# Operands of a routing search moved from SBUF to PSUM or to a per-partition scalar, in a kernel of attention and two mixtures of experts

## The chip, the cores and the metric

One core of a Trainium2 chip runs the whole program. The metric is device time in microseconds for one execution, from the inputs in HBM to the outputs in HBM. The core's engines are TensorE (PE in the rows), VectorE (DVE), ScalarE (ACT), GpSimd (POOL) and SyncE (SP), each with a queue of its own that it works off in order.

## The reference

Three layers run one after the other; what matters here is the third and how it assigns tokens.

```python
def _attn_ref(q, k, v, alpha):           # 4 x 8 heads, 768 tokens, 48 wide
    for t in range(S):
        state = alpha[:, :, t, :, None] * state + einsum('bhd,bhe->bhde', k[:, :, t], v[:, :, t])
        y[:, :, t] = einsum('bhd,bhde->bhe', q[:, :, t], state)

def _moe_ref(x, w_in, w_out):            # 3072 tokens, 384 -> 2048 -> 384
    h = np.maximum(x @ w_in, 0.0)
    return h * h @ w_out

def _moe2_ref(x, w_gate, w1, w2):        # 8 experts, 384 -> 1024 -> 384
    cap = N // E                         # 384 tokens for each expert
    logits = x @ w_gate
    for idx in np.argsort(-logits.flatten()):
        tok, e = idx // E, idx % E
        if assigned[tok] >= 0 or counts[e] >= cap: continue
        assigned[tok] = e; counts[e] += 1
    for e in range(E):
        h = np.maximum(x[assigned == e] @ w1[e], 0.0)
        out[assigned == e] = h @ w2[e]
```

The greedy loop goes through all pairs of token and expert from the greatest logit down; an expert with 384 tokens is closed.

## The kernel before

The first 597 us or so are attention and the first mixture, which the change does not touch. Then comes the routing, and with it, interleaved, the eight routed experts.

**The routing** works in phases, one for each expert that fills up (`search`, line 801). The logits `L` lie in SBUF as 128 partitions x 24 chunks x 8 experts. A phase looks for the greatest threshold at which some open expert would have 384 tokens whose best open logit is at or above it. It does so in 5 rounds (`ITERS`), each with 32 thresholds (`T`) in a finer grid:

- `thr` (line 827): the 32 thresholds, the round's grid `iot` plus the per-partition numbers `n` and `at`; in the first round they are the grid itself;
- `cm` (line 829): which of a partition's 24 tokens are at or above each threshold, 768 comparisons a partition of `m2` with `thr`, both spread by steps of zero;
- `pc` (838, TensorE): six products of `cm` with `oh`, each token's best expert, that count the tokens; `rc` (841) takes the counts to SBUF;
- `pb` (851): TensorE adds the blocks up; `full` (854) compares with what the experts still take; `pb` (856) counts how many thresholds are full, and `steps` (865) makes the next `n` of it;
- `at` (861): in the third and fourth round, one element a partition, the thresholds' offset so far plus `n`;
- in the second round `ee` (844) multiplies `oh` with the experts' numbers, both in SBUF, and in the third `ei` (847) adds that up.

Behind the fifth round, `hi` (869) is the threshold found, `a` (873) marks the tokens above it, and `aid` (874, a copy under the mask `a`) gives them their expert's number. TensorE's `pz`, then `cl`, `cz`, `ez` and `ek` (879 to 884) name the expert that closed; `mk`, `mi` and `wi` (885, 886, 705) list its tokens and where its weights lie, from which its weights (`w1s`, `w2s`) and, after `slots`, its tokens (`xg`) are fetched by indirect DMA from GpSimd's queue. `na` (896) takes the assigned tokens out of the next phase.

**The experts.** Each has 8 steps; a step is `layer1` (`ph`, line 957, nine products) and `layer2` of two steps before (`py`, line 975, three times three products). Weights and tokens are split into a high and a low part for float32 accuracy: ScalarE makes the high parts of the weights (line 920), GpSimd (or VectorE, where the plan says d) subtracts them from the whole to get the low ones (`wbuf`, line 922), with both inputs in SBUF; these come in short bursts. `xt` (931, 932) does the same for the tokens, on ScalarE and VectorE, out of PSUM.

**What sets the order.** From line 631 on, TensorE, VectorE, ScalarE and GpSimd work in the order of the program text. Tables written out by hand (`START`, `FIRST`, `STEADY`, `EXTRA` and their like, lines 51 to 82) say behind which product of an expert's step a piece of the search (`s`), of the slots (`t`), of the weights' split (`h` on ScalarE, `p` on GpSimd, `d` on VectorE) or of the tokens (`x`) is issued. So while expert e runs, phase e + 2 is searched, and a product for `pc` stands in TensorE's queue between those of the expert: what makes `cm` late makes the expert late.

**PSUM** has eight banks: three with the tag a (`bank("a", ...)`, line 96), taken in turn by the routing's tiles and the tokens' transposes, two for `ph`, three for `py`. Before the change `thr`, `at` and `a` lie in SBUF; a round's bank for `pc` is taken just before its products.

Of the kernel before, what the change touches and what calls it, by code (L numbers as in the profile page):

```python
# [7 lines left out]
F32 = mybir.dt.float32  # L8
# [5 lines left out]
OP = mybir.AluOpType  # L14
# [6 lines left out]
E, F2 = 8, 1024  # L21
CAP = N // E
C = 128
NCH = N // C
# [24 lines left out]
# what each step of an expert does beside its products: s the search of a phase after the next, t the slots  # L49
# of the next, h, p, d weights' parts, x tokens, e, w the former expert's results  # L50
# [37 lines left out]
def moe_kernel(ctx: ExitStack, tc: tile.TileContext, akq, v, w_in, w_out, w_gate, w1, w2, out,  # L88
# [14 lines left out]
    # the last chunk's rows come after one of zeros  # L103
# [14 lines left out]
    # attention inputs of one chunk of 128 tokens: decays, keys and queries with a pair of heads' columns in the  # L118
    # partitions, a column of zeros after each pair's tokens, and values with the tokens in the partitions
# [3 lines left out]
    def load(ch, parts=((0, 3),), eng=sp):  # L123
        """the rows between a pair's heads take the second's first, for whatever is finite will do"""
        for lo, hi in parts:
            for p0, n, r0 in ((0, 64, 0), (64, 48, 48)):
                eng.dma_start(nat[ch % 2][p0:p0 + n, lo:hi, :, :C], akq[ch, r0:r0 + n, lo:hi])
# [4 lines left out]
    # constants that the first chunk needs  # L132
# [30 lines left out]
    # constants that depend on shapes alone  # L163
# [45 lines left out]
    XF, XT = {}, {}  # L209

    def back(x):
        """a row's elements, the last one first"""
        n = x.shape[-1]
        return bass.AP(tensor=x.tensor, offset=x.offset + n - 1, ap=[list(a) for a in x.ap[:-1]] + [[-1, n]])

    def attn(ch, tags="aaaaa"):
        """yields after each of its parts: a decays, q queries and keys, s scores, n keys back, o results"""
# [7 lines left out]
        # products of the decays from each token on, and up to each token over the whole chunk's; what each pair's  # L225
        # start from comes in where the zeros are
# [41 lines left out]
        def result(lo, hi):  # L268
            """what some pairs of heads give, in one bank"""
            py = bank(next(tag), "py")  # L270
            o = py.rearrange("p (a t) -> p a t", a=NP)
            for p in range(lo, hi if c else lo):
                pe.matmul(o[:, p], sa[:, p], qt[:, p], start=p == lo, stop=False)
            for p in range(lo, hi):
                for j in range(2):
                    pe.matmul(o[64 * j:64 * j + D, p], vn[:, 2 * p + j], Pt[:, j, p, :],
                              start=not c and p == lo, stop=p == hi - 1)
            for h in ((slice(0, 128),) if c and hi == NP else (slice(0, D), slice(64, 64 + D))):
                act.activation(x[h, lo:hi, cu * C:(cu + 1) * C], v4(py)[h, lo:hi], AF.Copy)
            if cu == CPU - 1 and hi == NP:  # L280
                # the last pair of heads fills the rows that the other pairs leave
                for o in (0, 64):
                    sp.dma_start(x[o + 48:o + 64, :KT, :], x[o:o + 48, KT, :])
# [63 lines left out]
    def narrow(dst, src):  # L347
        """float64 words (low, high) to float32, of which dst takes the bits"""
# [82 lines left out]
    def gate(dst, x):  # L431
        """x's rows times the gate's weights"""
# [5 lines left out]
    def gate_w():  # L438
        """w_out's rows times the gate's weights"""
# [9 lines left out]
    def share(n):  # L449
        """n steps of what the vector engine does for the gate"""  # L450
        while n and tasks:
            if next(tasks[-1], "end") == "end":
                tasks.pop()
            else:
                n -= 1

# [14 lines left out]
    def start_conv(n=1):  # L471
        """the next conversions, in turns so that none waits for itself"""
# [44 lines left out]
    def logit_range():  # L517
        """the lowest of the logits, but for the last unit's, and what scales them from there to 0..T"""
# [25 lines left out]
    def attend(g):  # L544
        """attention's parts that go with step g"""
# [11 lines left out]
    def first_step(g):  # L557
        """a step of the first unit, whose weights come along"""
# [71 lines left out]
    # the rest, in the order of this text  # L630
# [3 lines left out]
    def last_unit():  # L634
        """the last unit's second layer, three products at a time"""
# [50 lines left out]
    # logits of the last unit  # L686
# [33 lines left out]
    def load_half(h):  # L720
        """half of the second layer's weights, for the first expert"""
# [10 lines left out]
    def slots(k, mk, mi, part=False):  # L732
        """token of each of the 384 slots of the expert whose tokens mk marks; mi counts them in a partition;
        in part: the last chunk's are not gathered but marked"""
# [57 lines left out]
    def prep(k):  # L792
        """what a phase's search starts from"""
# [7 lines left out]
    def search(k):  # L801
        """one phase: the greatest threshold with which an expert is full, that expert and its tokens"""
# [20 lines left out]
        for it in range(ITERS):  # L823
            thr = iot[:, 0]
            if it:
                thr = sm.tile([128, T], F32, name="thr", bufs=2)
# [8 lines left out]
            # G chunks at a time, of which the blocks on the diagonal count  # L835
            pc = bank("a", "pc")
# [22 lines left out]
            elif 1 < it < ITERS - 1:  # L859
                at2 = sm.tile([128, 1], F32, name="at", bufs=2)  # L860
                dve.tensor_tensor(at2, at, n, op=OP.add)  # L861
# [5 lines left out]
        # the threshold as the last comparison had it  # L867
# [4 lines left out]
        a = sm.tile([128, NCH], F32, name="a", bufs=2)  # L872
# [37 lines left out]
    def split_w(k, i, e="hp"):  # L910
        """a part of an expert's weights: three of the first layer's, four of the second's"""
# [22 lines left out]
    def first_x():  # L934
        """the first expert's tokens: those of the last chunk from where they are, and the others as they come"""
# [114 lines left out]
    # whether each phase closed one expert and each expert has its 384 tokens  # L1050
# [29 lines left out]
    def across(x, row, negate=False):  # L1080
        """the greatest of a column's values, in every partition"""
# [7 lines left out]
    def total(x, n):  # L1089
        """the sums of n columns over the partitions, in every partition"""  # L1090
# [6 lines left out]
    def general_phase(L2, gum, gaid, gcap, tok, idr):  # L1097
# [19 lines left out]
        # tokens with the same first choice that come before each token  # L1117
# [16 lines left out]
        # the last token of each expert that fills up, and the first of these tokens  # L1134
# [22 lines left out]
        # the tokens up to that one get their first choice  # L1157
# [59 lines left out]
def arrays(inputs):  # L1217
    """the inputs as the chip reads them"""
    import numpy as _np

    # a chunk's tokens last, a pair's heads before the pairs
# [3 lines left out]
    # rows in the order in which the attention's results come  # L1225
# [30 lines left out]
```

## Time and profile before

| | us |
|---|---|
| median of 3 runs | 973.15 |
| lowest and highest run | 966.78 and 974.82 |
| span of the profiled execution, for which no other time is given | 973.9 |
| busy in it: TensorE | 833.9 |
| busy in it: VectorE | 714.5 |
| busy in it: GpSimd | 443.2 |
| busy in it: ScalarE | 327.7 |

The span runs from the first to the last instruction of one execution. Busy times say how much of it an engine was at work, not who was waited for. An instruction that is held while it runs, by another engine's use of a port for instance, counts as busy: in the rows a long duration of a small instruction is such a hold. A timeline row gives the start, the duration, the engine, the line, the operation, its output and inputs, and in brackets the idle time before it and what ended that. Neighbouring instructions of one kind are merged into one row, with their number.

### The profile page before, as it was taken

What the parts mean: (1) busy time and instruction counts of PE and PEld (TensorE: products, weight loads), DVE (VectorE), ACT (ScalarE), POOL (GpSimd) and SP (SyncE); (2) the same over time, 40 slices, a digit from 0 to 9 for tenths busy, and PEclk for the clock granted to TensorE, in tenths of its full rate; (3) what the DMA queues carried; (4) which work ended last, traced back from release to release, by engine and by line L of the source; (5) the groups of instructions that cost most, each with busy time, mean ns of one, the idle gap of its engine ahead of it and who ended that gap; (6) DMA issues with size and microseconds to landing.
All of it is one profiled execution on the core that took longest, in us unless ns stands there. A gap on an engine that the chain in (4) does not pass through costs nothing.

```text
span 973.9 us, 14629 instructions
## 1 busy us (share of the span) xinstructions
PE 833.9 (86%) x5583; PEld 759.1 (78%) x5583; DVE 714.5 (73%) x1594; ACT 327.7 (34%) x581; POOL 443.2 (46%) x389
## 2 busy tenths in 40 slices
PE   6868779888979889899999999748788797988974
PEld 6658678877878779899999998647677685777974
DVE  6878998999998999958542134777687787875540
ACT  1344533223123223233343352224242442425521
POOL 2386763353454444433342442343464556644431
PEclk7888989999999999999999999958798898988988
DMA  9763543112122122232300000314042240422400
GB/s 208 156 190 107 164 110 70 37 28 61 38 43 62 37 43 61 37 72 56 58 25 1 7 25 13 134 37 155 1 178 102 77 171 9 178 84 96 179 25 27
DMA packets 51484, 76.98 MB, mean 79 GB/s; under 512 B 3409, under 2 KB 42706, under 8 KB 49362
## 3 DMA queue, kind: packets, MB, share of 16 engines
q1 hardware_dynamic: 21570, 27.24, 10.3%
q0 software_dynamic: 5520, 34.61, 9.6%
q10 hardware_dynamic: 24320, 14.16, 7.7%
q8 instruction: 45, 0.74, 0.3%
q14 instruction: 29, 0.24, 0.1%
HBM read 65.27 MB, written 9.54 MB: 77 GB/s over the span
## 4 chain that ended last, share of the span: by engine, by line
PE 40%; DVE 36%; issue 4%; ACT 4%; DMA 1%; POOL 1%; POOLq 0%; DVEq 0%; ACTq 0%
DVE gj L435 15%; PE ph L390 9%; PE p L414 7%; PE ph L957 7%; PE py L975 7%; DVE at L861 3%; PE p L641 3%; DVE s L400 3%; DVE wbuf L922 2%; ACT wbuf L920 2%; DVE A L232 1%; DVE thr L827 1%; DVE cm L829 1%; DVE suf L229 1%; DVE Pt L261 1%
## 5 line engine op out<-in xcount | busy, mean ns | idle before, releaser
L390 PE MATMUL ph<-xT,wbuf 128*128 128x384 f32 x1152 | 234.6, 348 | 29.5 <-DVE s L400 12.0
L390 PEld LDWEIGHTS ph<-xT,wbuf 128*128 128x128 f32 x1152 | 207.5, 192 | 40.4 <-DVE s L400 17.4
L402 POOL TENSOR_TENSOR hl<-s,hl 128x384 fp32r<-128x384 f32 x112 | 141.8, 1266 | 184.9 <-ACT hl L401 171.2
L414 PE MATMUL p<-wbuf,hl 128*128 128x384 f32 (+1 forms) x1008 | 205.4, 348 | 4.9 <-POOL hl L402 2.7
L414 PEld LDWEIGHTS p<-wbuf,hl 128*128 128x128 f32 x1008 | 180.0, 193 | 12.2 <-issue 4.2
L975 PE MATMUL py<-wbuf,hl 128*128 128x384 f32 x576 | 133.6, 364 | 0.0
L957 PE MATMUL ph<-xt,wbuf 128*128 128x384 f32 x576 | 122.5, 358 | 10.3 <-DVE xt L932 5.9
L400 DVE SCALAR_TENSOR_TENSOR s<-ph,s 128x384 f32<-128x384 f32 x112 | 62.0, 553 | 89.2 <-ACT s L395 88.8
L401 ACT ACTIVATE hl<-s 128x384 fp32r<-128x384 f32 x112 | 58.8, 525 | 195.7 <-DVE s L400 193.8
L957 PEld LDWEIGHTS ph<-xt,wbuf 128*128 128x128 f32 x576 | 103.7, 198 | 14.1 <-DVE xt L932 6.7
L975 PEld LDWEIGHTS py<-wbuf,hl 128*128 128x128 f32 x576 | 105.6, 201 | 0.7
L435 DVE SCALAR_TENSOR_TENSOR gj<-gx,wg 128x384 f32<-128x384 f32 x128 | 96.1, 751 | 3.1
L395 ACT ACTIVATE s<-ph 128x384 f32<-128x384 f32 x128 | 62.1, 486 | 100.2 <-PE ph L390 70.5
L435 DVE SCALAR_TENSOR_TENSOR gj<-xo,wg 128x384 f32<-128x384 f32 x120 | 78.3, 652 | 12.9 <-ACT xo L422 10.5
L965 ACT ACTIVATE hl<-ph 128x384 fp32r<-128x384 f32 x64 | 31.7, 496 | 135.6 <-PE ph L957 118.6
L922 POOL TENSOR_TENSOR wbuf<-w2s,wbuf 128x768 fp32r<-128x768 f32 x28 | 53.3, 1925 | 44.1 <-ACT wbuf L920 44.1
L966 DVE SCALAR_TENSOR_TENSOR hl<-ph,hl 128x384 fp32r<-128x384 f32 x64 | 35.4, 553 | 38.3 <-ACT hl L965 37.4
L920 ACT ACTIVATE wbuf<-w1s 128x1024 fp32r<-128x1024 f32 x24 | 52.2, 2227 | 2.3 <-DMA w1s<-in_moe_w_dram,wi 2.3
L983 POOL DMA_INDIRECT out_dram<-o,idx x24 | 29.8, 1243 | 50.9 <-ACT o L980 19.0
L838 PEld LDWEIGHTS <-cm 128*128 128x128 bf16 x210 | 8.1, 100 | 49.9 <-DVE cm L829 46.3
L838 PE MATMUL pc<-oh,cm 128*128 128x32 bf16 x210 | 11.3, 182 | 40.1 <-DVE cm L829 40.1
L729 POOL DMA_INDIRECT xg<-x2d,row x24 | 25.1, 1046 | 38.7 <-DVE idx L785 18.2
(204 smaller groups left out, 1229.8 us busy)
## 6 DMA issues: line engine op xcount, KB each, us to landing
rawi<-in_moe_w_in_dram SPq DMA_DIRECT2D x16, 384.0 KB, 3.5
rawo<-in_moe_w_out_dram SPq DMA_DIRECT2D x16, 384.0 KB, 3.7
akq<-in_akq_dram ACTq DMA_DIRECT2D x16, 384.0 KB, 4.5
akq<-in_akq_dram ACTq DMA_DIRECT2D x16, 288.0 KB, 5.8
x2d<-xo SPq DMA_DIRECT2D x24, 192.0 KB, 2.0
v<-in_v_dram ACTq DMA_DIRECT2D x16, 192.0 KB, 2.5
akq<-in_akq_dram SPq DMA_DIRECT2D x7, 384.0 KB, 5.8
akq<-in_akq_dram SPq DMA_DIRECT2D x7, 288.0 KB, 7.3
```

Of the source, the lines that this page charges most:

```text
L390: pe.matmul(ph[:, :UT], win[:, wi, kt, fs], XT[u][:, xi, kt, :], start=n == 0, stop=n == 3 * KT - 1)
L395: act.activation(s, ph[:, :UT], AF.Relu)
L400: dve.scalar_tensor_tensor(s, ph[:, :UT], 0.0, s, op0=OP.max, op1=OP.mult)
L401: act.activation(hl[:, 0], s, AF.Copy)
L402: (dve if (u, f) == (NU - 1, FT - 1) else pool).tensor_tensor(hl[:, 1], s, hl[:, 0].bitcast(F32), op=OP.subtract)
L414: pe.matmul(PY[u][t][:, :w], hl[:, si, t * C:(t + 1) * C], wout[:, wi, f, :w], start=f == 0 and n == 0, stop=f == FT - 1 and n == 2)
L435: dve.scalar_tensor_tensor(junk, x, 1.0, wg[:, e], op0=OP.mult, op1=OP.mult, accum_out=dst[:, e:e + 1])
L920: act.activation(dst[:, 0], src, AF.Copy)
L922: (dve if "d" in e else pool).tensor_tensor(dst[:, 1], src, dst[:, 0].bitcast(F32), op=OP.subtract)
L957: pe.matmul(ph[:, :CAP], wa[:, wi, kt, j, :], xt[:, xi, kt, :], start=n == 0, stop=n == 3 * KT - 1)
L966: dve.scalar_tensor_tensor(hl[:, 1], ph[:, :CAP], 0.0, hl[:, 0].bitcast(F32), op0=OP.max, op1=OP.subtract)
L975: pe.matmul(PX[k, i][:, :DM], hl[:, hi_, i * 128:(i + 1) * 128], wb[:, wi, j, :], start=j == 0 and n == 0, stop=j == FT2 - 1 and n == 2)
```

## The change

Four operands of the search move; everything is computed as before.

- `thr` lies in the round's PSUM bank `pc`, in the 32 columns behind those of the counts, and the bank is taken at the start of the round.
- `cm` thereby compares `m2` in SBUF with `thr` in PSUM.
- `at` is made by a `tensor_scalar`, with `n` as a per-partition scalar, in place of a `tensor_tensor` with two tensor inputs.
- `a` lies in the last round's bank `pb`, behind the columns of the counts; `aid` and `na` read it there.

```diff
         for it in range(ITERS):
+
+            pc = bank("a", "pc")
             thr = iot[:, 0]
             if it:
-                thr = sm.tile([128, T], F32, name="thr", bufs=2)
+                thr = pc[:, G * E:G * E + T]
                 dve.tensor_scalar(thr, iot[:, it], n, at, op0=OP.add, op1=OP.add)
             cm = sm.tile([128, NCH, T], BF, name="cm", bufs=2)
             dve.tensor_tensor(cm, m2[:, :, None].to_broadcast([128, NCH, T]),
...
             yield
-            pc = bank("a", "pc")
             for c in range(0, NCH, G):
...
                 at2 = sm.tile([128, 1], F32, name="at", bufs=2)
-                dve.tensor_tensor(at2, at, n, op=OP.add)
+                dve.tensor_scalar(at2, at, n, None, op0=OP.add)
                 at = at2
...
-        a = sm.tile([128, NCH], F32, name="a", bufs=2)
+        a = pb[:, 2 * E:2 * E + NCH]
         dve.tensor_scalar(a, m2, hi, None, op0=OP.is_ge)
         dve.copy_predicated(aid, a.bitcast(mybir.dt.uint32), ei)
```

The rest of the diff takes comments out. No instruction moves: every engine has as many as before, in the same order, and only the operands of those above differ. Behind the changed lines the numbers go up by one (`cm` is line 831, `at` 862, `a` 874 and `aid` 875 of the kernel after).

## Rows read from the trace of the kernel before

**Rows 1.** Page, part 4: share of the chain that ended last, by engine.

```profile
PE 40%; DVE 36%; issue 4%; ACT 4%; DMA 1%; POOL 1%; POOLq 0%; DVEq 0%; ACTq 0%
```

**Rows 2.** Waits from 628 us on: us in total, times, longest us.

```profile
PE pc L838 <- DVE cm L829: 40.1, 11, 9.7
...
PE pp L736 <- DVE wi L705: 3.2, 6, 1.0
```

**Rows 3.** Instructions of three tiles: ns min/median/max, first and last start us, forms.

```profile
L861 DVE TENSOR_TENSOR at<-n x7: 138/6627/6705, 608.7 to 847.7; 128x1 f32<-128x1 f32 x7
...
L827 DVE TENSOR_SCALAR thr<-iot,n,zero x7: 300/302/8439, 601.9 to 839.1; 128x32 f32<-128x32 f32 x7
...
L829 DVE TENSOR_TENSOR cm<-m,thr x28: 957/958/3540, 602.3 to 860.6; 128x768 bf16<-128x768 f32 x28
```

**Rows 4.** Timeline of the first of four like stalls: start us, us, what.

```profile
723.69 5.82 POOL L922 TENSOR_TENSOR wbuf<-w1s,wbuf 128x1024 fp32r<-128x1024 f32 x2
724.11 0.56 DVE L932 TENSOR_TENSOR xt<-px,xt 128x384 fp32r<-128x384 f32 x1 [0.45 <-ACT xt L931]
...
724.66 6.63 DVE L861 TENSOR_TENSOR at<-n 128x1 f32<-128x1 f32 x1
...
729.46 1.80 POOL L922 TENSOR_TENSOR wbuf<-w2s,wbuf 128x768 fp32r<-128x768 f32 x1
...
732.76 0.34 PE L838 MATMUL pc<-oh,cm 128*128 128x32 bf16 x6 [5.38 <-DVE cm L829]
...
736.82 2.10 PE L957 MATMUL ph<-xt,wbuf 128*128 128x384 f32 x9
```

**Rows 5.** A subtraction of 384 columns with both inputs in SBUF, GpSimd idle.

```profile
L402 DVE TENSOR_TENSOR deferred<-s,deferred x1: 559/559/559, 593.5 to 593.5; 128x384 fp32r<-128x384 f32 x1
```

**Rows 6.** Timeline of the next burst on GpSimd, and of VectorE beside it.

```profile
737.89 5.83 POOL L922 TENSOR_TENSOR wbuf<-w2s,wbuf 128x768 fp32r<-128x768 f32 x3 [6.62 <-ACT wbuf L920]
...
739.96 0.18 DVE L841 CAST rc<-pc 128x32 f16<-128x32 f32 x1
...
741.52 0.27 DVE L869 TENSOR_SCALAR hi<-n,at 128x1 f32<-128x1 f32 x1
...
741.84 1.92 DVE L873 TENSOR_SCALAR a<-m,hi 128x24 f32<-128x24 f32 x1
...
744.75 0.17 DVE L883 SCALAR_TENSOR_TENSOR ez<-cz,ioe 128x8 f32<-128x8 f32 x1
```

**Rows 7.** Window behind the stall: busy us by engine, PEclk, DMA share, GB/s.

```profile
734.00:736.80 2.80, 2.80 (x14) 1.91 (x12) 1.13 (x3) 1.30 (x3) 0.00 (x0) 0.50 0.00 0
```

**Rows 8.** Timeline of the same products at the full clock, one expert earlier.

```profile
693.14 0.32 PE L838 MATMUL pc<-oh,cm 128*128 128x32 bf16 x6
...
695.59 1.83 PE L957 MATMUL ph<-xt,wbuf 128*128 128x384 f32 x9
```

**Rows 9.** Timeline of the stall in the expert before that.

```profile
678.69 6.08 POOL L922 TENSOR_TENSOR wbuf<-w1s,wbuf 128x1024 fp32r<-128x1024 f32 x2 [1.65 <-ACT wbuf L920]
...
679.34 2.68 DVE L827 TENSOR_SCALAR thr<-iot,n 128x32 f32<-128x32 f32 x1
...
682.05 3.54 DVE L829 TENSOR_TENSOR cm<-m,thr 128x768 bf16<-128x768 f32 x1
684.70 2.57 POOL L922 TENSOR_TENSOR wbuf<-w2s,wbuf 128x768 fp32r<-128x768 f32 x1
...
685.65 0.34 PE L838 MATMUL pc<-oh,cm 128*128 128x32 bf16 x6 [5.81 <-DVE cm L829]
...
689.18 3.25 PE L957 MATMUL ph<-xt,wbuf 128*128 128x384 f32 x9
```

**Rows 10.** Timeline of the first stall, before the first expert's products.

```profile
633.80 8.44 DVE L827 TENSOR_SCALAR thr<-iot,n,zero 128x32 f32<-128x32 f32 x1
...
636.87 5.31 POOL L922 TENSOR_TENSOR wbuf<-w2s,wbuf 128x768 fp32r<-128x768 f32 x3
...
643.77 0.35 DVE L844 TENSOR_TENSOR ee<-oh,ioe 128x192 f32<-128x192 bf16 x1
```

## The prediction

> **What bounds the kernel now.** I read the chain of waits first. TensorE has 40% of it and VectorE 36% [rows 1]: for long stretches the end is set by VectorE. The change touches the routing alone, which begins some 375 us before the end, so the waits of that stretch came next. There TensorE waits 40.1 us in 11 pieces for `cm`, the comparison with which each round of the search begins, the longest 9.7 us; and 3.2 us in 6 pieces for `wi`, which stands behind the end of a search [rows 2].
>
> Why is `cm` late? The list of durations answers it [rows 3]. The sum `at` is one element a partition; its shortest run took 138 ns, and its median is 6,627 ns. `thr` goes from 300 to 8,439 ns, `cm` from 957 to 3,540 ns. Nothing in their sizes differs; something holds them. The timeline of one expert shows what [rows 4]: GpSimd begins three subtractions of weight parts (`wbuf`) at 723.69 and ends the last at 729.46 + 1.80 = 731.26; `at`, begun at 724.66, ends at 731.29. In that burst `xt`, with one input in PSUM and one in SBUF, took 0.56 us, what the same size takes with both inputs in SBUF and nobody beside it (559 ns, [rows 5]). In the next burst, from 737.89 to 743.72, `rc` (from PSUM to SBUF) took 0.18 us and `hi` 0.27 us, while `a`, with 24 elements, was held for 1.92 us, to the end of that burst [rows 6]. So what is held has two tensor inputs in SBUF (`at`, `cm`), or is a `tensor_scalar` from SBUF to SBUF with more than one element (`thr`, `a`). What passes has an input in PSUM (`xt`, `rc`), or is a one-element `tensor_scalar` with per-partition scalars (`hi`).
>
> The Trainium skill (SBUF — State Buffer, Who interferes with whom) says this as a rule: VectorE and GpSimd share a pair of ports, taken for a whole instruction by a VectorE instruction with two SBUF inputs or one in a two-port mode. The trace agrees, with 6.63 us for one element.
>
> **The change part by part.** The order of the instructions is the same on every engine; only where operands lie changes. `at` becomes the kind of instruction that `hi` is. `thr` writes PSUM, which no row shows for an SBUF input; its bounds are 0.30 us, the free run, and a hold as today. I take the free run: its mirror image `rc`, with only the other side in PSUM, is the nearest row and passes. `cm` takes one input from PSUM and becomes the kind that `xt` is: free, at 0.96 us. `a` and `aid` likewise. What remains as it was is `ee`, two SBUF inputs, once a search.
>
> *The four steady stalls.* `at` is held in four experts (at 724.66, 765.8, 806.7 and 847.7 us), and each time TensorE waits some 5.38 us for `cm` [rows 4]. TensorE is done with its products at 732.76 − 5.38 = 727.38. Without the hold `at` ends at 724.9, `steps` and `thr` take half a microsecond and `cm` ends by 726.8: before TensorE asks. The wait goes whole. Its cost goes on behind it, because TensorE comes out of it at a granted clock of 0.50, the 1.2 GHz level [rows 7]. From the products for `pc` to the next expert's first `ph` it then takes 736.82 − 732.76 = 4.06 us; the same products at the full clock, an expert earlier, took 695.59 − 693.14 = 2.45 [rows 8]. That is 1.61 us, and 2.10 − 1.83 = 0.27 on `ph` itself. Per expert 5.38 + 1.61 + 0.27 = 7.26; four times, 29.0.
>
> What is late next? That `ph` needs the parts GpSimd is still making. Its first two subtractions end at 723.69 + 5.82 = 729.51; TensorE will be there at 727.38 + 2.45 = 729.83. So the wait stays away by 0.3 us, and GpSimd is the next bound. The second burst waits for ScalarE, which follows TensorE, and moves along.
>
> *The stall at 679.* `thr` waits for GpSimd's first subtraction, `cm` for its second, and `cm` ends at 685.59; TensorE has waited 5.81 us, since 679.84 [rows 9]. Free, `thr` and `cm` take 679.34 + 0.30 + 0.03 + 0.96 = 680.6, and 0.95 us of waiting is left with the semaphores: 4.86 saved. The clock: 689.18 − 685.65 = 3.53 against 2.45, and `ph` 3.25 against 1.83, together 2.50. But GpSimd's two subtractions end at about 678.69 + 5.8 = 684.5, and `ph` would be due at 680.8 + 2.45 = 683.25; some of its products can go ahead, so 0.9 us is given back. 4.86 + 2.50 − 0.9 = 6.5.
>
> *The stall at 633.8.* Here `thr` is held 8.44 us, through GpSimd's burst up to 636.87 + 5.31 = 642.18 [rows 10]. Free, `cm` would end near 635.1 and TensorE's products and `rc` near 635.6. Then comes `ee`, which still has two SBUF inputs, in the middle of the same burst. `full` and all further products of TensorE stand behind it. If it is held to the end of the burst it ends at 642.53; before it ended at 643.77 + 0.35 = 644.12: a gain of 1.6 us. If it gets in at the first change of instruction (636.87), the gain is 644.12 − 636.87 − 0.3, less a little, or 7.0 us. I take 1.6: `thr` missed three such changes in this very burst (before each of the last three subtractions), and `at` missed two in each of its four.
>
> *The end of a search.* `a` and `aid` no longer hold `wi`. TensorE's 3.2 us there [rows 2] don't go whole, since `pz` and `hl` stand in between: half, 1.5.
>
> *Costs.* `cm`'s 768 columns against the 384 of [rows 5] give (957 − 559) / 384 = 1.04 ns a column; were `thr` to pay that in full for its 32 columns on top of what it costs today, it would be 33 ns a round, under 1 us in all, and mostly hidden beside TensorE's products. A page speaks against the change here: the Trainium skill (VectorE: DVE Perf Modes, The TRN2 errata) gives VectorE a fixed 120 cycles from PSUM against 58 from SBUF. By that, an estimate, some 65 ns on each `thr` and `cm` of some 24 rounds among the experts is 3 us, and the sum would end near 938. The rows differ: 0.56 us with PSUM [rows 4] against 0.559 without [rows 5]. I take nothing, neither a loss nor a gain.
>
> Sum: 29.0 + 6.5 + 1.6 + 1.5 = 38.6. From the span of the profiled execution, 973.9 us, that leaves 935.3. The median of the three runs is 973.15, 0.1% below the span, so no correction: 935 us.
>
> **Rivals.**
>
> *The hold lasts one GpSimd instruction only.* Then `ee` passes at 636.87, the first stall gives 7.0 in place of 1.6, and the time is 930. For it: at 679 `thr` and then `cm` got in between two of GpSimd's instructions, and GpSimd's third took 2.57 us there [rows 9] against 1.80 [rows 4]. Against: the eight changes that `at` missed. The Trainium skill (SBUF — State Buffer, Who interferes with whom) has the loser blocked until the first finishes; [rows 4] show it blocked past two finishes.
>
> *GpSimd, or a slow clock, keeps half of it.* The margin before `ph` is 0.3 us. If the subtractions lengthen, if `ez` (two SBUF inputs), which began 744.75 − 743.72 = 1.03 us behind the second burst's end [rows 6] and comes closer as `a` gets shorter, runs into that burst at one subtraction, 1.8 us, a time, or the clock stays low so that the 10 us counted for it don't come, it costs 4 × 1.8 = 7 and up to 10 us: 942 to 952, 947 in the middle. For it: how thin the margins are.
>
> *`thr` is held even with its output in PSUM.* Then `at` passes but `thr` ends where `at` did, at 731.3 + 0.3, and `cm` at 732.6, where it ended at 732.7. The steady stalls stay. What is left is `cm` at 682.05, 3.54 − 0.96 = 2.6, and part of 1.5: 970, no change that can be told. Against it: `rc`.
>
> *Slower: `cm` reads PSUM slowly.* Its second input repeats 32 PSUM columns 24 times, which no row shows. The gain is used up from 38.6 / 24 = 1.6 us more on each of the 24 `cm` among the experts, so from 2.6 us each. At four times the present 0.96 it would be 24 × 2.88 = 69 us, and the time 973.9 − 38.6 + 69 = 1004. Against it: `xt` reads 384 PSUM columns at the usual pace.
>
> **How the numbers follow.** My forecast has 0.55, the shorter hold 0.20, half kept 0.15, `thr` still held 0.06, the slow read 0.04. The first three are faster by over 1% (below 963.4, about what a measurement of this kernel can tell from no change): 0.90. The fourth is the same, 0.06, the last slower, 0.04. The range goes down to 926, which is 930 with the 3 us of TensorE's shorter waits for `cm` (40.1 − 9.7 − 5.8 − 4 × 5.4) and the 0.9 given to GpSimd, and up to 952, the third case's upper end.
>
> **What would show it.** In the list of durations `at`, `thr`, `cm`, `a` and `aid` should have maxima near their medians. TensorE's wait for `cm` should fall from 40.1 to under 12 us, and the four pieces of 5.4 should be gone, with the granted clock at 1.00 behind them. `ee` (0.35 us where nothing holds it, [rows 10]) should have one run of over 6 us near 636, which is new; if it is about 1.3 us, the first rival is right. I am wrong if `thr` shows runs of several microseconds again, if `cm` is over 1.1 us, or if the waits for `cm` go and the time stays above 955.

## The result, and the profile after

The kernel after takes 926.84 us (median of 4 runs, 924.29 to 930.47), the kernel before 973.99 us beside it (4 runs, 966.78 to 977.53): a ratio of 0.9546, with a 95% interval of 0.9493 to 0.9598. A ratio, here and below, is to runs of the kernel before that were taken beside it, from undisturbed runs alone, so it is not the quotient of the two medians. The forecast was 935 us, 926 to 952. The profiled execution's span fell from 973.9 to 924.4 us.

I read the same views as before. First the chain by engine, from the page of the kernel after, part 4; against [rows 1] VectorE's share falls from 36% to 31%:

```profile
PE 41%; DVE 31%; ACT 6%; issue 3%; DMA 2%; POOL 1%; POOLq 0%; ACTq 0%; DVEq 0%
```

The waits from 628 us on (total, times, longest), against [rows 2]:

```profile
PE pc L839 <- DVE cm L831: 5.3, 6, 1.6
...
PE pp L736 <- DVE wi L705: 1.6, 6, 0.3
```

TensorE's wait for `cm` went from 40.1 to 5.3 us, and no piece of 5.4 us is left. The durations (ns, min/median/max), against [rows 3]:

```profile
L829 DVE TENSOR_SCALAR pc<-iot,n,zero x7: 314/314/315, 600.9 to 799.5; 128x32 f32<-128x32 f32 x7
...
L831 DVE TENSOR_TENSOR cm<-m,pc x28: 953/954/955, 601.2 to 814.3; 128x768 bf16<-128x768 f32 x28
...
L845 DVE TENSOR_TENSOR ee<-oh,ioe x7: 348/348/608, 603.7 to 801.3; 128x192 f32<-128x192 bf16 x7
...
L862 DVE TENSOR_SCALAR at<-n x7: 192/192/193, 607.7 to 808.1; 128x1 f32<-128x1 f32 x7
...
L875 DVE COPY_PREDICATED aid<-pb,ei x7: 186/188/190, 616.0 to 818.2; 128x24 f32<-128x24 uint32 x7
```

The maximum of every changed instruction is at its median (for `a`, now named `pb`, 248 and 246 ns); `ee`, which was not changed, has one run of 608 ns. By the medians `thr` (now named `pc`) costs 314 ns instead of 302, `cm` 954 instead of 958. The timeline of a steady expert, against [rows 4], shows them inside GpSimd's burst:

```profile
704.78 0.99 POOL L984 DMA_INDIRECT out_dram<-o,idx  x1 [2.42 <-ACT wbuf L921]
705.79 6.06 POOL L923 TENSOR_TENSOR wbuf<-w1s,wbuf 128x1024 fp32r<-128x1024 f32 x2
...
707.88 0.19 DVE L862 TENSOR_SCALAR at<-n 128x1 f32<-128x1 f32 x1
...
708.56 0.31 DVE L829 TENSOR_SCALAR pc<-iot,n,at 128x32 f32<-128x32 f32 x1
708.91 0.95 DVE L831 TENSOR_TENSOR cm<-m,pc 128x768 bf16<-128x768 f32 x1
...
710.44 0.32 PE L839 MATMUL pc<-oh,cm 128*128 128x32 bf16 x6
...
712.88 1.83 PE L958 MATMUL ph<-xt,wbuf 128*128 128x384 f32 x9
```

`cm` ends at 709.86, TensorE's products for `pc` start at 710.44 with no wait in brackets, and 2.44 us later comes `ph`, in 1.83 us: the pace of the full clock [rows 8]. The window around it confirms that (PEclk is the number before the last two, 1.00, where [rows 7] had 0.50):

```profile
710.40:714.00 3.60, 3.60 (x31) 3.03 (x30) 2.35 (x9) 2.34 (x5) 3.24 (x2) 1.00 0.00 0
```

Where did the time go, stretch by stretch? The product `pp` comes once an expert, so the times at which it starts cut the span into stretches. The same one before and after:

```profile
745.69 0.17 PE L736 MATMUL pp<-mi,onesb 128*128 128x24 bf16 x1 [0.56 <-DVE wi L705]
```

```profile
721.18 0.17 PE L736 MATMUL pp<-mi,onesb 128*128 128x24 bf16 x1 [0.27 <-DVE wi L705]
```

| stretch | before, us | after, us | gain | forecast |
|---|---|---|---|---|
| start to the first `pp` | 619.3 | 618.2 | 1.0 | 0 |
| to the second (stall at 633.8) | 44.6 | 37.7 | 6.9 | 1.6 |
| to the third (stall at 679) | 40.7 | 31.9 | 8.8 | 6.5 |
| four steady experts | 163.9 | 133.6 | 30.4 | 29.0 |
| to the last `pp` | 35.2 | 31.9 | 3.3 | 0 |
| to the end | 70.1 | 71.0 | -0.9 | 0 |

The gains add up to 49.5 us, the difference of the two spans. The forecast's further 1.5 us, for the ends of the searches, lies within these rows. Four questions were left for the chip: which of the edits does it, whether the forms are held as I said, why `ee` was not held, and what decides whether a held instruction gets in early.

### The profile page after: what moved, and what is told of

The parts are those of the page before. It is cut to its first block, busy times and chain, and to the rows that moved or that the text cites. A ratio compares the mean times of both kernels' runs of the same rounds, so it can differ in the third digit from the quotient of the medians.

```text
span 924.4 us, 14629 instructions
## 1 busy us (share of the span) xinstructions
PE 818.3 (89%) x5583; PEld 745.2 (81%) x5583; DVE 666.8 (72%) x1594; ACT 326.7 (35%) x581; POOL 436.9 (47%) x389
## 4 chain that ended last, share of the span: by engine, by line
PE 41%; DVE 31%; ACT 6%; issue 3%; DMA 2%; POOL 1%; POOLq 0%; ACTq 0%; DVEq 0%
DVE gj L435 17%; PE ph L390 9%; PE ph L958 9%; PE p L414 7%; PE py L976 7%; ACT wbuf L921 3%; DVE s L400 3%; DVE wbuf L923 2%; PE p L641 2%; DMA w1s<-in_moe_w_dram,wi 2%; DVE A L232 2%; DVE suf L229 1%; DVE Pt L261 1%; PE py L276 1%; DVE hl L967 1%
## 5 line engine op out<-in xcount | busy, mean ns | idle before, releaser
L390 PEld LDWEIGHTS ph<-xT,wbuf 128*128 128x128 f32 x1152 | 204.6, 190 | 41.9 <-DVE s L400 17.0
L976 PE MATMUL py<-wbuf,hl 128*128 128x384 f32 x576 | 127.2, 351 | 0.0
L976 PEld LDWEIGHTS py<-wbuf,hl 128*128 128x128 f32 x576 | 100.7, 191 | 0.7
L984 POOL DMA_INDIRECT out_dram<-o,idx x24 | 27.3, 1138 | 51.4 <-ACT o L981 19.7
L232 DVE TENSOR_TENSOR_SCAN A<-akq,whole 112x515 f32<-112x515 f32 x24 | 42.2, 1757 | 0.5
L923 POOL TENSOR_TENSOR wbuf<-w1s,wbuf 128x1024 fp32r<-128x1024 f32 x13 | 39.4, 3051 | 6.3 <-ACT wbuf L921 6.2
L729 POOL DMA_INDIRECT xg<-x2d,row x24 | 22.9, 954 | 38.7 <-DVE idx L785 18.1
```

The lines of the kernel that those rows point to most:

```text
L232: dve.tensor_tensor_scan(one(A)[:, :-1], one(al)[:, :-1], whole[:, 1:-1], whole[:, 0:1], op0=OP.mult, op1=OP.add)
L390: pe.matmul(ph[:, :UT], win[:, wi, kt, fs], XT[u][:, xi, kt, :], start=n == 0, stop=n == 3 * KT - 1)
L923: (dve if "d" in e else pool).tensor_tensor(dst[:, 1], src, dst[:, 0].bitcast(F32), op=OP.subtract)
L976: pe.matmul(PX[k, i][:, :DM], hl[:, hi_, i * 128:(i + 1) * 128], wb[:, wi, j, :], start=j == 0 and n == 0, stop=j == FT2 - 1 and n == 2)
```

## The experiments

**One edit undone at a time.** First `at`:

```diff
-                dve.tensor_scalar(at2, at, n, None, op0=OP.add)
+                dve.tensor_tensor(at2, at, n, op=OP.add)
```

> The kernel after, with the one-element sum at as a tensor_tensor again; thr and a stay in PSUM. Theory (at, with two inputs in SBUF, is held by GpSimd's subtractions and nothing else in the steady stalls needs help): the four steady stalls come back and the two others do not. In the steady experts at runs about 6 us instead of 0.19, TensorE waits about 5.4 us for cm, an expert takes about 40.7 us instead of 33.4, and the time is 926.8 + 4 x 7.3 = 956 us (951 to 960). Rival (the gain came from the PSUM operands, and at was only late with the rest): at passes now that thr and cm do, and the time stays at 926 to 932.

Measured: 956.47 us (4 runs, 952.68 to 958.33), 0.9834 of before (0.9759 to 0.9909). Two rows of the durations, and TensorE in the first steady stall:

```profile
L862 DVE TENSOR_TENSOR at<-n x7: 136/5623/6252, 602.3 to 828.1; 128x1 f32<-128x1 f32 x7
...
L845 DVE TENSOR_TENSOR ee<-oh,ioe x7: 348/348/6753, 598.3 to 821.2; 128x192 f32<-128x192 bf16 x7
...
714.81 0.33 PE L839 MATMUL pc<-oh,cm 128*128 128x32 bf16 x6 [4.38 <-DVE cm L831]
```

The theory holds: a sum of one element a partition, in the wrong form, costs 30 us, of which the four steady experts have 27 in the profiled run. TensorE's waits there are 4.4 to 5.0 us, a little under the 5.4 expected. Not expected was that the stretch with the stall at 633.8 took 41.3 us, where the kernel after has 37.7: `ee`, which passed in 0.61 us in the kernel after, was held for 6.75 us here though nothing on it differs. That question comes back below.

Next `thr` in SBUF again, by which `cm` has two SBUF inputs as well:

```diff
-                thr = pc[:, G * E:G * E + T]
+                thr = sm.tile([128, T], F32, name="thr", bufs=2)
```

> The kernel after, with thr in SBUF again, so that cm has two SBUF inputs again; at stays a tensor_scalar and a stays in PSUM. Theory (the hold moves to the next held form): at passes in 0.2 us, thr, begun 0.7 us later, is held to the end of the same burst, some 5 us, so all six stalls are as long as in the kernel before: 926.8 + 4 x 7.3 + 8.8 + 7 = 972 us (966 to 976). Rival (at alone was the cause in the steady stalls): they stay away, only the stalls at 679 and 634 come back, 926.8 + 8.8 + 7 = 943 us.

Measured: 968.86 us (10 runs, 957.08 to 978.30), 0.9958 of before (0.9916 to 1.0): with `at` free and `thr` not, hardly anything is left of the gain. The hold moves on to the next held form. In the profiled execution, the fastest of the ten, the time between two `pp` was 41.1, 35.7, 40.3 and 37.2 us in the four steady experts, so two of the stalls were long and two short. One of each kind:

```profile
717.36 5.88 POOL L923 TENSOR_TENSOR wbuf<-w1s,wbuf 128x1024 fp32r<-128x1024 f32 x2
...
719.01 6.03 DVE L829 TENSOR_SCALAR thr<-iot,n,at 128x32 f32<-128x32 f32 x1
...
756.64 0.96 DVE L831 TENSOR_TENSOR cm<-m,thr 128x768 bf16<-128x768 f32 x1
757.50 5.98 POOL L923 TENSOR_TENSOR wbuf<-w1s,wbuf 128x1024 fp32r<-128x1024 f32 x2
...
760.14 0.39 DVE L829 TENSOR_SCALAR thr<-iot,n,at 128x32 f32<-128x32 f32 x1
760.56 3.74 DVE L831 TENSOR_TENSOR cm<-m,thr 128x768 bf16<-128x768 f32 x1
```

At 719.01 `thr` waits out the whole burst; at 760.14 it is let in at GpSimd's first change of instruction, and `cm` at the next. What differs is that at 757.50 a `cm` with two SBUF inputs was still running when the burst began.

Then `cm` alone, with `thr` made in PSUM and copied to SBUF:

```diff
                 dve.tensor_scalar(thr, iot[:, it], n, at, op0=OP.add, op1=OP.add)
+                thr, thr_p = sm.tile([128, T], F32, name="thr", bufs=2), thr
+                dve.tensor_copy(thr, thr_p)
```

> The kernel after, with thr made in PSUM as there and then copied to SBUF (32 columns, one more VectorE instruction of about 0.18 us), so that cm has two SBUF inputs; tells what cm's own form is worth. Theory (cm is held by its own two SBUF inputs): thr and the copy pass, cm is held to the end of the burst, some 4 to 5 us, and the steady stalls come back: 926.8 + 4 x 7 + 5 to 10 for the other two = 958 to 968 us. Rival (only thr was held, cm is late because thr is): 926.8 + 24 copies of 0.2, mostly hidden, 927 to 932 us.

Measured: 962.36 us (4 runs, 956.55 to 968.55), 0.9868 of before (0.9777 to 0.9959). `thr` (0.31 us) and the copy pass inside the burst, `cm` is held:

```profile
718.56 0.19 DVE L831 COPY thr<-pc 128x32 f32<-128x32 f32 x1
718.78 6.24 DVE L833 TENSOR_TENSOR cm<-m,thr 128x768 bf16<-128x768 f32 x1
```

So the three edits of the search's head only work together: each form left as it was keeps most of the stall.

Last `a`:

```diff
-        a = pb[:, 2 * E:2 * E + NCH]
+        a = sm.tile([128, NCH], F32, name="a", bufs=2)
```

> The kernel after, with a in SBUF again. Theory: a, begun about 2 us before the end of the second burst, is held again for about 1.9 us in the steady experts instead of 0.25, and TensorE's wait in front of pp grows by a few tenths of a microsecond a search: 0 to 3 us in all, 927 to 930. Rival (ez comes into the burst or the clock falls behind it, so that the end of a search weighs as much as the start): 934 us or more.

Measured: 927.79 us (4 runs, 925.34 to 930.87), 0.9524 of before (0.9450 to 0.9598), which cannot be told from the kernel after. `a` gets in at a change of instruction, and `aid`, whose mask now lies in SBUF, takes over the hold:

```profile
L874 DVE TENSOR_SCALAR a<-m,hi x7: 227/440/455, 614.6 to 817.8; 128x24 f32<-128x24 f32 x7
L875 DVE COPY_PREDICATED aid<-a,ei x7: 191/1770/1775, 614.8 to 818.3; 128x24 f32<-128x24 uint32 x7
```

In the profiled execution an expert took 33.8 us between two `pp` instead of 33.4, some 2 us in all. The `a` edit is in the direction I said, and too small for this measurement.

**Each form by itself.** A kernel of bursts alone, with one VectorE instruction in each (code shortened):

```python
for i in range(3):
    pool.tensor_tensor(lo[:, i], src, hi[:, 0], op=OP.subtract)   # 128x1024, all in SBUF
act.activation(x, src[:, 0:T], AF.Copy)                           # starts the VectorE instruction
last = f(x, y)                                                    # one of 14 forms
```

> No part of the reference is computed: bursts of three GpSimd subtractions of 128x1024 with both inputs in SBUF, some 9 us each, and one VectorE instruction started by ScalarE inside each burst, at three delays, in 14 forms; before that each form once without a burst. Theory (a VectorE form is held if it has two tensor inputs in SBUF, or is a many-element one-input instruction from SBUF to SBUF): held for microseconds are at as tensor_tensor, thr and a into SBUF, cm with thr in SBUF, aid with its mask in SBUF, ee, ez and the two-element tensor_scalar; not held, within 30 ns of the time without a burst, are at as tensor_scalar, thr and a into PSUM, cm and aid out of PSUM, and the reduction ei. First rival (any instruction that touches only SBUF is held): at as tensor_scalar and ei are held too. Second rival (only two tensor inputs in SBUF are held): thr and a into SBUF and the two-element tensor_scalar pass. When a held one gets in: if at each end of a GpSimd instruction, no hold is over 3.1 us; if only at the burst's end, holds are up to 8 us and shrink with the delay.

Measured, as min/median/max with 1 run alone and 3 inside bursts (for `at_tt` and `thr_sb` 3 more, in bursts whose inputs ScalarE made one by one); `_sb` and `_ps` say where the output of `thr` and the second input of `cm` lie:

```profile
L121 DVE TENSOR_TENSOR at_tt<-sc,x x7: 129/865/1672, 5.6 to 390.7; 128x1 f32<-128x1 f32 x7
...
L126 DVE TENSOR_SCALAR at_ts<-sc,x x4: 211/212/214, 6.1 to 63.5; 128x1 f32<-128x1 f32 x4
...
L131 DVE TENSOR_SCALAR thr_sb<-src,x,sc x7: 300/884/1695, 6.7 to 415.6; 128x32 f32<-128x32 f32 x7
...
L136 DVE TENSOR_SCALAR thr_ps<-src,x,sc x4: 312/314/315, 7.4 to 113.3; 128x32 f32<-128x32 f32 x4
...
L146 DVE TENSOR_TENSOR cm_ps<-m,y x4: 953/954/955, 9.5 to 165.4; 128x768 bf16<-128x768 f32 x4
...
L175 DVE TENSOR_REDUCE ei<-x x4: 185/186/188, 14.0 to 315.1; 128x8 f32<-128x32 f32 x4
...
L185 DVE TENSOR_SCALAR ts<-x,sc x4: 228/1476/1677, 15.2 to 364.9; 128x2 f32<-128x2 f32 x4
```

All 14 forms do what the theory says; those not shown are `a` (held into SBUF, free into PSUM), `cm` with `thr` in SBUF, `ee` and `ez` (held), and `aid` (held with its mask in SBUF, 188 ns out of PSUM). The first rival falls with `at_ts` and `ei`, which touch SBUF alone and pass. The second falls with `ts`: two elements of one input are held, one element is not. But no hold was over 1.7 us: here a held instruction always got in at the next change of GpSimd's instruction, where `at` in [rows 4] missed two.

**What decides when a held instruction gets in.** In the steady stalls GpSimd goes straight from the DMA of a result into the burst (704.78 and 705.79 above, 20 ns apart); in the kernel of forms it waited for ScalarE in front of each burst. So, with and without such a DMA (code shortened):

```python
pool.indirect_dma_start(out=xg, out_offset=None, in_=w2r, in_offset=...)   # in half of the bursts
for i in (0, 1, 2)[::flip]:
    pool.tensor_tensor(lo[:, i], src, hi[:, 0], op=OP.subtract)
```

> No part of the reference is computed: 48 bursts of three GpSimd subtractions of 128x1024, and in each one VectorE instruction of a held form (at as tensor_tensor, thr into SBUF, cm with thr in SBUF), started by ScalarE at four delays, some 0.2 to 3.5 us behind the burst's start. Half of the bursts come after GpSimd has waited for ScalarE, half directly behind an indirect DMA that GpSimd issues; in each half, half with a contiguous and half with a strided source, as for the first layer's weights. It asks when a held instruction gets in. First theory (a burst directly behind a GpSimd DMA lets nobody in, as in 17 of 20 such holds of the six traces so far): behind a wait all get in at the next change, holds at most 3.0 us; behind a DMA they are held to the burst's end, up to 8 us. Second theory (the strided source does it): the holds to the end stand in the strided groups alone. Third (neither; it is decided by something else in the whole kernel): all get in at the next change, in all four groups.

Measured: the first theory, in 48 of 48 bursts. One behind a wait, one behind a DMA, both with the strided source, the instruction some 1 to 3 us into the burst:

```profile
285.69 8.45 POOL L216 TENSOR_TENSOR wlo<-wide,whi 128x1024 f32<-128x1024 f32 x3 [1.33 <-ACT row L212]
...
288.92 2.46 DVE L131 TENSOR_SCALAR thr_sb<-src,x,sc 128x32 f32<-128x32 f32 x1 [10.12 <-ACT x L223]
...
402.96 0.96 POOL L208 DMA_INDIRECT xg<-in_moe_w_dram,row  x1 [1.69 <-ACT row L207]
403.94 8.44 POOL L216 TENSOR_TENSOR wlo<-wide,whi 128x1024 f32<-128x1024 f32 x3
...
404.88 7.55 DVE L131 TENSOR_SCALAR thr_sb<-src,x,sc 128x32 f32<-128x32 f32 x1 [3.56 <-ACT x L223]
```

Six of the 24 instructions behind a DMA began 0.15 to 0.31 us before the burst, while the DMA was still being issued, and were held all the same.

Does it hold in the whole kernel? There a break was put between DMA and burst, in the kernel with `at` back and, as a control, in the kernel after:

```diff
+                        if a == "p2" and (r, p) == (6, 4):
+                            z = [sm.tile([128, 1], F32, name=f"z{i_}", bufs=1) for i_ in range(3)]
+                            pool.memset(z[0], 0.0)
+                            act.activation(z[1], z[0], AF.Copy)
+                            pool.tensor_tensor(z[2], z[1], z[0], op=OP.subtract)
                         split_w(k, i, a[:-1])
```

> The kernel with at back as a tensor_tensor (956.5 us median), and in front of each burst that follows an output DMA of GpSimd a break: GpSimd sets one element, ScalarE copies it, GpSimd waits for that and subtracts one element, then begins the burst, some 0.6 us later. It asks whether the rule of the small bursts (a held instruction gets in at the next change of instruction where GpSimd has waited in front of the burst, and at the burst's end where it came straight from an indirect DMA) decides the steady stalls of the whole kernel. Theory: at is held 1 to 3 us instead of 5.6 to 6.3, to the end of the first subtraction; TensorE waits about 1 us or less for cm instead of 5.0; 956.5 - 4 x 6 = 932 us (927 to 938). Rival (in the whole kernel something else decides): at stays at 5.6 us or more and the time at 953 to 960.

> The kernel after with the same break, as a control: what the break itself costs. Theory: the burst begins some 0.6 us later and TensorE's next ph waits for it by at most that, four times: 927 to 930 us. Rival (the break delays ScalarE and with it TensorE): 932 us or more, which is to be taken off the run with at back.

Measured: with `at` back 940.69 us (4 runs, 935.50 to 944.59), 0.9669 of before (0.9614 to 0.9725), where it was 0.9834 without the break; the control 927.75 us (4 runs, 926.85 to 928.87), 0.9525 (0.9474 to 0.9576), so the break itself costs a microsecond at most. `at` is held, in each of the five experts with this burst, exactly to the end of the first subtraction:

```profile
705.15 5.91 POOL L923 TENSOR_TENSOR wbuf<-w1s,wbuf 128x1024 fp32r<-128x1024 f32 x2
...
705.41 2.83 DVE L862 TENSOR_TENSOR at<-n 128x1 f32<-128x1 f32 x1
...
709.72 0.32 PE L839 MATMUL pc<-oh,cm 128*128 128x32 bf16 x6 [1.58 <-DVE cm L831]
```

The hold is as the theory says; the time is 9 us above its 932, outside the range expected. In the profiled run, the fastest of the four, TensorE still waits 1.6 us each time instead of under 1, and the steady experts take 35.2 us and, where the granted clock is 0.95 instead of 1.00, 36.6 and 36.7. The control's take 33.9 to 34.0, and one, at 0.95, 36.9. These are some 5 us; where the rest lies is not shown.

What ends it, the wait or the instruction in between? The code is shortened:

```python
if case == "memset":
    pool.memset(z, 0.0)                       # between DMA and burst, no wait
if case == "wait":
    act.activation(hi[:, 0], src, AF.Copy)    # the burst waits for this
if case == "cross":
    f_cm_sb(x0, None)                         # two cm beside the DMA, over the burst's start
    f_cm_sb(x0, None)
```

> No part of the reference is computed: 20 bursts of three GpSimd subtractions of 128x1024, each with a VectorE instruction of a held form (at as tensor_tensor, thr into SBUF) started inside it. Five cases of four bursts: straight behind an indirect DMA of GpSimd; behind such a DMA and a one-element memset of GpSimd, without a wait; behind such a DMA and a wait for ScalarE; straight behind the DMA, but with two cm with thr in SBUF running on VectorE when the burst begins; and straight behind a plain DMA that GpSimd issues. It asks what in front of a burst makes the hold last to its end. Theory (GpSimd takes the way into SBUF for the DMA and keeps it while it has something to do; any wait, for ScalarE or for VectorE, ends that): held to the burst's end (4 to 7 us) in the first, second and fifth case, to the next change of instruction (under 2.5 us) in the third and fourth. Rival (only the instruction just in front counts): the second case is let in at the next change, the fourth is held to the end.

Measured: the theory, in 20 of 20. The instruction in the case with a memset, with the wait, and with `cm` across the start:

```profile
47.29 6.06 DVE L121 TENSOR_TENSOR at_tt<-sc,x 128x1 f32<-128x1 f32 x1 [3.56 <-ACT x L231]
...
100.36 1.54 DVE L121 TENSOR_TENSOR at_tt<-sc,x 128x1 f32<-128x1 f32 x1 [11.69 <-ACT x L231]
...
129.60 2.04 DVE L121 TENSOR_TENSOR at_tt<-sc,x 128x1 f32<-128x1 f32 x1 [0.20 <-ACT x L231]
```

Behind a plain DMA of GpSimd the holds were 4.8 to 5.9 us, to the burst's end as well. The last of the three rows fits the short stalls of the run with `thr` back; GpSimd's DMA took 1.68 us there instead of 0.96, so GpSimd itself was kept waiting. In the ten traces of whole kernels (before, after and eight experiments) I count 67 holds of over 0.15 us with a change of GpSimd's instruction still ahead: behind a wait 34 got in at the first change and 2 did not (one began 0.04 us before it, the other stays unexplained), straight behind a DMA 28 were held to the burst's end and 3 got in, all three with a `cm` running free across the burst's start. That alone is not enough: in the run with `cm` held, one `cm` that began 0.55 us before such a burst, at 838.33, was itself held, for 8.8 us.

**A faster version.** In the kernel after one held instruction still makes TensorE wait for microseconds, a weight part that the plan of the last two experts gives to VectorE:

```profile
875.68 5.10 DVE L923 TENSOR_TENSOR wbuf<-w2s,wbuf 128x768 fp32r<-128x768 f32 x1
...
881.77 0.69 PE L958 MATMUL ph<-xt,wbuf 128*128 128x384 f32 x1 [3.43 <-DVE xt L933]
```

```diff
-(6, 5, "d3 p4")
+(6, 5, "p3 p4")
```

> The kernel after, with one weight part of the last two experts (the fourth of seven, 768 columns, both inputs in SBUF) subtracted by GpSimd instead of VectorE, in the same place of the program: the one held VectorE instruction that TensorE still waits behind for microseconds. Theory: in the last expert it was held for 5.10 us, xt behind it came 3.8 us late and TensorE waited 3.4 us for it; without it that wait goes, and in the expert before 0.2 to 0.7 us: 926.8 - 3.6 = 923 us (922 to 925). Rival (GpSimd has one subtraction more in front of the parts that TensorE needs next, so the wait only changes its name): 926 to 930 us.

Measured: 921.58 us (6 runs, 912.18 to 922.47), 0.9446 of before (0.9395 to 0.9497): the theory, and a microsecond more. In the profiled run TensorE no longer waits for that `xt`. The same with `ee` out of PSUM:

```diff
+                ip = pc[:, G * E + T:G * E + T + E]
+                dve.tensor_copy(ip, ioe)
-                dve.tensor_tensor(ee, oh, ioe[:, None, :].to_broadcast(eb), op=OP.mult)
+                dve.tensor_tensor(ee, oh, ip[:, None, :].to_broadcast(eb), op=OP.mult)
```

> The kernel with the weight part on GpSimd (the run before: 921.6 us median, 912 to 922), and besides ee, the last instruction with two SBUF inputs in a search's middle, reads the experts' numbers from PSUM: 8 columns copied there in front of it, into the round's bank. Theory: ee is 0.35 us in every search, whatever GpSimd does. Where it had got in at the first change anyway (0.62 us in the profiled runs of this kernel and of the kernel after), that is worth 0.3 us less the copy's 0.15, so the median stays within 2 us, 920 to 923; where it had been held for the whole burst, as in the run with at back (6.75 us), it is worth 5.4 us, and runs at the upper end of the spread go. Rival (ee's hold decides the spread of the runs): median and lowest both near 916.

Measured: 918.01 us (6 runs, 914.91 to 922.89), 0.9430 of before (0.9390 to 0.9471). `ee` is at most 355 ns. The median is below the 920 to 923 of the theory and above the rival's 916. Against the run just above, the medians differ by 3.6 us, but the ranges overlap, so what `ee` adds stays open. No run of either version is as slow as the fastest of the kernel after (924.29 us); they were not taken beside it, and the intervals of the first version's ratio and of its own just touch (0.9497 and 0.9493).

## Why the prediction was right, and where it was not

By the spans the gain was 49.5 us where I had summed 38.6: 5.3 more at the stall at 633.8, 2.3 more at 679, 3.3 before the last `pp`. So the time came out near the lower end of the range: by the forecast's mechanism, in one place by the first rival's, and with some luck in two places, as told below.

**What is held.** Right, in all 14 forms. The line that I drew from a handful of rows (two tensor inputs in SBUF, or a many-element `tensor_scalar` from SBUF to SBUF) stands, with `aid` and its mask in SBUF on the held side.

**The four steady stalls, 29.0.** Measured 30.4: 7.6 an expert instead of 7.26, and most of the difference is TensorE's wait before `pp`, 0.27 us instead of 0.56 above, which I had counted with the ends of the searches. The parts are those of the prediction: the wait of 5.38 is gone, and from `pc` to `ph` TensorE takes 2.44 us (forecast 2.45). The margin to GpSimd, which I put at 0.3, was 712.88 - (705.79 + 6.06) = 1.03 us, since the output DMA in front of the burst took 0.99 us instead of 1.51 and the burst began 4.65 us before TensorE's products instead of 3.69. So the rival of GpSimd or a slow clock as next bound did not come.

**The stall at 679, 6.5.** Measured 8.8. The wait fell from 5.81 to 0.85, by 4.96 (forecast 4.86). The clock was mis-sized: from one `pc` to the next TensorE took 693.14 - 685.65 = 7.49 us, and now 4.36, so 3.13 instead of 2.50; I had compared with a round that has a transpose more. And "0.9 us is given back" was wrong:

```profile
670.77 6.33 POOL L923 TENSOR_TENSOR wbuf<-w1s,wbuf 128x1024 fp32r<-128x1024 f32 x2 [1.71 <-ACT wbuf L921]
...
672.74 0.32 PE L839 MATMUL pc<-oh,cm 128*128 128x32 bf16 x6 [0.85 <-DVE cm L831]
...
674.90 1.83 PE L958 MATMUL ph<-xt,wbuf 128*128 128x384 f32 x9
...
677.10 0.32 PE L839 MATMUL pc<-oh,cm 128*128 128x32 bf16 x6
```

This `ph` runs at full pace while GpSimd is still at the parts: it is the former expert's last step and does not need them. The remaining 0.7 us is the end of the search and what I don't resolve.

**The stall at 633.8, 1.6.** This step failed; the gain was 6.9, the first rival's 7.0. I had `ee` held to the end of the burst because `thr` had missed three changes in the same burst. The timeline after:

```profile
629.69 0.94 POOL L722 DMA_INDIRECT w2s<-in_moe_w_dram,wi  x1 [0.30 <-issue]
...
633.68 2.85 POOL L923 TENSOR_TENSOR wbuf<-w1s,wbuf 128x1024 fp32r<-128x1024 f32 x1 [3.05 <-ACT wbuf L921]
...
636.14 0.61 DVE L845 TENSOR_TENSOR ee<-oh,ioe 128x192 f32<-128x192 bf16 x1
```

It was no longer the same kind of burst: the DMA of `w2s` ended 3 us before the burst, GpSimd waited for ScalarE, and `ee` got in at the first change. In the run with `at` back the burst came straight from that DMA, and `ee` was held for 6.75 us, as I had said; that stretch took 41.3 us, 3.3 less than before. So the first rival was right on this stall, and its rule (one GpSimd instruction only) holds where GpSimd has waited; in the steady stalls it does not.

Which kind of burst it was turned on a fraction of a microsecond in front of it. In the kernel before, VectorE began a weight part, with two SBUF inputs, just ahead of GpSimd's third DMA for `xg`:

```profile
629.27 2.00 DVE L922 TENSOR_TENSOR wbuf<-w1s,wbuf 128x1024 fp32r<-128x1024 f32 x1 [0.98 <-issue]
...
629.50 2.54 POOL L729 DMA_INDIRECT xg<-x2d,row  x1 [0.30 <-issue]
```

The issue of that DMA took 2.54 us instead of 0.95, and the DMA of `w2s` behind it ended at 634.05, 0.02 us ahead of the burst. The run with `at` back had the same order, by 0.08 us. In the kernel after, VectorE began this part at 629.75, behind the third DMA for `xg` (628.44), and the seven other traces have that order too, once by 0.01 us. The change touches none of these instructions, and no run shows that it decides their order. So the 3.6 us that this stretch gained beyond the 3.3 are luck, as far as can be told.

The Trainium skill (SBUF — State Buffer, Who interferes with whom) has the engine that starts first keep the ports for its whole instruction. Behind a wait the traces agree: `at` is let in 2.83 us after its start, at the end of the first subtraction. Straight behind a GpSimd DMA they differ, with 5.6 to 6.7 us over three instructions, and the measurement decides.

**The end of the search, 1.5.** About right: TensorE's wait for `wi` fell by 1.6, from 3.2 to 1.6 us.

**PSUM costs nothing.** Right, but for 12 ns on `thr`: 314 against 302 ns, and 954 against 958 for `cm`; the slow read did not come. The Trainium skill's fixed 120 cycles from PSUM against 58 from SBUF (VectorE: DVE Perf Modes, The TRN2 errata) would have been, by an estimate from it, 65 ns more on `cm`. The traces don't agree, as `cm` is no longer than it was. The prediction put these 65 ns on `thr` too, which was wrong: that rule is on a source in PSUM, and `thr` reads SBUF and writes PSUM, for which the small kernel shows 14 ns (`thr_ps` 314 against `thr_sb` 300, each alone).

**Not foreseen: 3.3 us before the last `pp`.** A weight part on VectorE, outside the edits, took 2.50 us instead of 4.28 in the next to last expert, which is over half of it. This too looks like luck: in the run with `a` back and in the one with `at` back and the break, the same part took 5.1 us, straight behind a DMA, and the stretch 35.7 and 36.1 us, as long as before. Without both pieces of luck the gain would be, by an estimate from these spans, 49.5 - 3.6 - 3.3 = 42.6 us, nearer to the 38.6. The rest of the table, +1.0 and -0.9, is within what the traces differ by: the first `pp` came between 612.8 and 620.9 us in the ten of whole kernels.

## What to carry to other kernels

An instruction of VectorE that takes microseconds instead of a tenth of one is worth a look at what GpSimd does beside it: give an instruction with two tensor inputs one of them in PSUM, give a `tensor_scalar` its output in PSUM, or make a one-element sum a `tensor_scalar` with a per-partition scalar, for under 0.1 us an instruction here (`at` 0.19 us instead of 0.14, `thr` 0.314 instead of 0.302). Do so for all instructions of a chain, since one that is left takes over the whole hold. And look at what stands in front of GpSimd's burst: straight behind a DMA that GpSimd issued, the hold is the rest of the burst and not of one instruction.

## What was not expected of the hardware

GpSimd's subtractions let a held VectorE instruction in at the next change of instruction, unless they come straight behind a DMA that GpSimd issued, indirect or plain; then they keep it out to the end of the burst, in all 24 such bursts of the small kernel, where an instruction of `cm`'s form took up to 9.4 us, and in 28 of 31 holds of the whole kernels. A memset between does not end that, a wait of GpSimd does, for ScalarE or while VectorE itself holds the way in. Why is not shown; that GpSimd takes the ports for the DMA and keeps them while it has something to do would fit nearly all of it, though not the one unexplained hold behind a wait.
